# Products with V in a visit of their own, and the first block's loads and ScalarE order

## The chip, the cores and the metric

The kernel runs on one core of a Trainium2 chip. TensorE (PE) multiplies matrices into PSUM, VectorE (DVE) and ScalarE (ACT) do the elementwise work, GpSimd (POOL) and SyncE (SP) here only issue DMAs, which move data between HBM and SBUF or within SBUF. Each engine works through its own instructions in order and waits on semaphores for the others. The metric is device time in microseconds (us), the median of three runs: lower is better.

## The reference

Attention with a relative-position bias, then two gated feed-forward layers, all in float32, with 4 batches, 8 heads, 576 positions, head size 64, so 2304 tokens of 512:

```python
scores = scale * np.matmul(q, k.transpose(0, 1, 3, 2))
x = (psi_rel / psi_i)[..., None]          # logs of |i-j| and of i
bias = np.maximum(x @ w1 + b1, 0.0) @ w2  # hidden 32, then 8 heads
scores = scores + bias.transpose(2, 0, 1)[None, :, :, :]
scores = scores - np.max(scores, axis=-1, keepdims=True)
attn = np.exp(scores)
attn = attn / (np.sum(attn, axis=-1, keepdims=True) + 1e-09)
x = np.matmul(attn, v)                    # to 2304 x 512
x = (1 / (1 + np.exp(-(x @ w_gate))) * (x @ w_val)) @ w_out   # d_ff 1536
h = x @ w_in                              # d_ff 2048
out = (h * np.clip(h + 3.0, 0.0, 6.0) / 6.0) @ w_out2
```

## The kernel before

**Tiling.** The 576 query positions are cut into five chunks (`QC`): four of 128 and one of 64 positions, each with all four batches, so 512 tokens (256 in the last). For each chunk there is attention, done unit by unit (`units`), and a block of 68 weight steps (`STEPS`: G and V are the two halves of the first layer, Y its output, H and O the second layer). Attention of chunk c + 1 runs beside the weight steps of chunk c. A lead computes chunk 0's attention alone. A unit is one pair of heads and one batch (two batches in the last chunk).

**A weight step** (`moe_step`, `product`, L496) is 12 matmuls of 128x512: every operand is split into a high and a low float32r part, and three of the four cross products are summed. ScalarE and VectorE then make the gate and split the result again (L505, L507, L523, L527, L532, L533). Weights come from HBM, 512 KB a step (`w_load`, L422 in the first block, L426 later). In the first block they are also converted from packed float64 and split (`w_split`, L466 to L477) and stored for the later blocks (`w_store`, L482).

**Attention of chunks 2 to 4** goes by pairs of units. `pair_qk` computes the scores of both (L368, L374 in the last chunk). `pair_soft` adds the bias and finds the minimum of the negated scores (L390), exponentiates (L256), normalises (L269) and transposes 32x32 blocks into `t` (L295). `pair_turn` copies `t` into `pT` by sixteen DMAs (L305), from GpSimd, or in chunk 2 half of them from SP. `pair_av` multiplies with V (L326, 40 matmul records a pair), and `att_x` splits the sum (L346, L347). Attention of chunks 0 and 1 (`att_qk` to `att_av`, L231 to L326) transposes on TensorE instead (L282) and copies with ScalarE (L285).

**What sets the order.** `block` walks through the weight steps and calls the events of `block_events` that are due at or before a step. The events of chunk 1 come from `chunk_att`, those of chunks 2 to 4 from `chunk_pairs`, and the bias of the next chunks from `chunk_bias` (L124, L126 on ScalarE and VectorE, L135 on TensorE). TensorE takes its instructions in the order written, and in the lead and the first block SP does too. ScalarE and VectorE after the lead, and SP after the first block, are ordered by the framework's scheduler. `issue_after` (L624, L625) holds everything written after the lead behind one instruction on the named engine: `gate` is a V load on SP, `gate_act` an instruction on ScalarE.

**Buffers.** PSUM: two double banks for scores (`ps_s`), four banks for everything else (`ps_m`). In SBUF, after the first block: `k` 4, `v` 4, `s` 2, `t` 1, `pT` 1, weights `wp` 6, so a weight load can be at most six steps ahead.

Of the kernel before, what the change touches and what calls it, by code (L numbers as in the profile page):

```python
# [56 lines left out]
def fused_kernel(ctx: ExitStack, tc: tile.TileContext, qd, kd, vd, tz, rd, zc, w2b, iden, wpack, out):  # L57
# [215 lines left out]
    def att_tr(u, part, mm_ps):  # L273

        d = st[u]
        if part == 0:
            d["pt"] = A["pt"].tile([128, 9, NQ], F32, name="pT")
        p = d["s"].rearrange("p h j -> p (h j)")
        ps = mm_ps()
        for t in range(3):  # L280
            k = 3 * part + t
            nc.tensor.transpose(  # L282
                out=ps[:, t * NQ:t * NQ + NQ], in_=p[:, 128 * k:128 * k + 128], identity=id_t
            )
        issued[1] = nc.scalar.activation(  # L285
            out=d["pt"][:, 3 * part:3 * part + 3],
            in_=ps[:, 0:3 * NQ].rearrange("p (t n) -> p t n", t=3), func=AF.Copy,
        )
# [43 lines left out]
    def att_x(u, po=None):  # L332
# [10 lines left out]
                xy_p.tile([128, NTOK], F32R, name="xyl"),  # L343
            )
        xh, xl = (x[:, b * n:b * n + w] for x in xs[c, hp])
        nc.scalar.activation(out=xh, in_=po[:, 0:w], func=AF.Copy)  # L346
        nc.vector.tensor_tensor(out=xl, in0=po[:, 0:w], in1=xh.bitcast(F32), op=ALU.subtract)  # L347


# [215 lines left out]
    with ExitStack() as lead:  # L565
# [23 lines left out]
        for n in range(NL + 2):  # L589
# [19 lines left out]
                w_part((n - 4) // 6, (n - 4) % 6)  # L609
            if n == NL - 4:  # L610
                gate = issued[0]
            if n == NL - 1:
                gate_act = issued[1]

    def late(name, bufs):
# [29 lines left out]
    def chunk_att(c, t0, t1, lag):  # L645

        us = units[c]
        d = (t1 - t0) / (len(us) - 1 + lag)
        ev = [(t0 - 2 * d, lambda: att_load(us[0], False)), (t0 - d, lambda: bias_read(us[0]))]
        for i, u in enumerate(us):  # L650
            a = t0 + d * i

            def first(u=u, nxt=us[i + 1] if i + 1 < len(us) else None):
                if nxt:
                    load_rows(nxt)
                    load_k(nxt)
                att_qk(u)
                att_min(u)
                att_exp(u)
                att_norm(u)  # L660
# [5 lines left out]
            ev.append((a, first))  # L666
        return ev

    def chunk_pairs(c, t0, t1):

        us, fast = units[c], c in (2, 3)
        ps = [tuple(us[i:i + 2]) for i in range(0, len(us), 2)]
        d = (t1 - t0) / len(ps)
        ev = [(t0 - min(d, 8), lambda: [att_load(u) for u in ps[0]])]
        for i, p in enumerate(ps):
            a = t0 + d * i

            def first(p=p, prev=ps[i - 1] if i else None, nxt=ps[i + 1] if i + 1 < len(ps) else ()):
                if prev:
                    pair_av(prev)  # L680
                pair_qk(p)
                pair_soft(p, 0)
                for u in nxt:
                    att_load(u)

            ev.append((a, first))
            ev.append((a + 1.5, lambda p=p: pair_soft(p, 1)))
            if fast:
                ev.append((a - min(d / 2, 3), lambda p=p: [att_split(u) for u in p]))
        ev.append((t1, lambda: pair_av(ps[-1])))  # L690
        return ev

    def block_events(k):
        ev = []
        last = NSTEP - 1
        if k == 0:
            ev += chunk_bias(1, 2.0, 1.5, NG1)
            ev += chunk_att(1, 15.5, last, 2)
        elif k == 1:
            ev += chunk_bias(2, 2.0, 1.5)  # L700
            d = (last - 21.0) / 8
            ev += chunk_pairs(2, 21.0, last)
            ev += chunk_bias(3, 24.5 - d / 2 - 1 + d, d / 2)
        elif k + 1 < NC:
            ev += chunk_pairs(k + 1, 0.5, last)
            if k == 2:
                d = (last - 0.5) / 8
                ev += chunk_bias(4, 4.5 - d - 1 + d, d)
        return [e[::2] for e in sorted((e[0], n, e[1]) for n, e in enumerate(ev))]

    def block(k):
# [87 lines left out]
```

## Time and profile before

| what | value |
|---|---|
| median of 3 runs | 1185.09 us (1185.08 to 1187.76) |
| profiled execution | 1188.6 us, its span 1186.8 us |
| TensorE matmul busy | 1121.2 us (94% of the span) |
| VectorE busy | 681.4 us (57%) |
| ScalarE busy | 528.4 us (45%) |
| mean granted TensorE clock | 0.977 |
| mean rate of the DMA engines | 271 GB/s |

A share of busy time is a mean over stages. The stages here are the lead (0 to 92.1 us from the span's start) and the five blocks of weight steps, which start at 92.1, 354.4, 616.1, 874.7 and 1084.2 us. The profile names a wait after the instruction or DMA that ended it. A granted clock of 1.0 is 2.4 GHz, one of 0.5 is 1.2 GHz.

### The profile page before, as it was taken

Reading aid. Unit: us, or ns where it says so; the run is one execution under the profiler, and the core shown is the slowest. Engines: PE = TensorE matmul, PEld = TensorE weight load, DVE = VectorE, ACT = ScalarE, POOL = GpSimd, SP = SyncE. Lnnn points to the kernel's source line nnn. Section 1 sums busy time; section 2 is a strip of 40 time slices with the busy share of each in tenths; the row PEclk is TensorE's granted clock in tenths of the full one; section 3 lists DMA queues with packets and bytes.
Section 4 is the critical chain, followed back from the end, with each engine's and each line's share of the span. In section 5 each row is a group of like instructions: output and inputs, shape, how many; then the busy total and the mean of one; then the engine's idle time right before and its main releaser. Section 6 shows DMA issues by size and latency. Waiting matters only on the chain.

```text
span 1186.8 us, 20167 instructions
## 1 busy us (share of the span) xinstructions
PE 1121.2 (94%) x7316; PEld 907.0 (76%) x7316; DVE 681.4 (57%) x1536; ACT 528.4 (45%) x1042; POOL 127.7 (11%) x260
## 2 busy tenths in 40 slices
PE   7989989999999999989988988998899999999998
PEld 3767667777777777767767876877677887889998
DVE  7897898899844456875644644654442515341232
ACT  7786777788843334543412422433211303231231
POOL 0000000000000011122112222222212112020000
PEclk9899999999999999999999999998899999999999
DMA  6946999999877778878787878786679889687997
GB/s 207 343 168 246 341 389 396 348 337 378 306 260 249 250 238 265 280 220 280 254 261 224 269 220 262 215 247 187 186 233 281 263 241 284 205 235 258 360 369 273
DMA packets 126610, 321.25 MB, mean 271 GB/s; under 512 B 25520, under 2 KB 40240, under 8 KB 126512
## 3 DMA queue, kind: packets, MB, share of 16 engines
q1 hardware_dynamic: 117888, 300.99, 75.0%
q0 software_dynamic: 8192, 18.89, 6.1%
q8 instruction: 58, 0.95, 0.3%
q14 instruction: 40, 0.33, 0.1%
q10 hardware_dynamic: 432, 0.09, 0.0%
HBM read 244.73 MB, written 50.99 MB: 249 GB/s over the span
## 4 chain that ended last, share of the span: by engine, by line
PE 64%; DVE 12%; DMA 12%; issue 3%; SPq 2%; POOL 2%; ACT 2%; DVEq 0%; ACTq 0%; POOLq 0%
PE ps L496 45%; PE ps L326 9%; DMA pT<-t 8%; PE ps L231 3%; PE ps L282 3%; DVE t L295 3%; DVE s L390 3%; PE ps L135 3%; POOL pT L305 2%; SPq L305 2%; DMA wp<-wsp 2%; DVE s L269 2%; PE ps L368 2%; DMA wd<-wpack 2%; DVE kl L212 1%
## 5 line engine op out<-in xcount | busy, mean ns | idle before, releaser
L496 PE MATMUL ps<-xyh,wp 128*128 128x512 f32 (+1 forms) x1600 | 469.7, 373 | 6.3 <-DVE tmp L527 2.9
L496 PEld LDWEIGHTS ps<-xyh,wp 128*128 128x128 f32 x1600 | 292.0, 190 | 66.2 <-issue 6.7
L496 PE MATMUL ps<-gh,wp 128*128 128x512 f32 (+1 forms) x1120 | 330.1, 372 | 0.0
L496 PE MATMUL ps<-xyl,wp 128*128 128x512 f32 (+1 forms) x800 | 296.5, 371 | 0.7 <-DVE xyl L509 0.7
L496 PEld LDWEIGHTS ps<-gh,wp 128*128 128x128 f32 x1120 | 203.4, 189 | 38.6 <-issue 3.7
L305 POOL DMA_DIRECT2D pT<-t x256 | 127.5, 505 | 925.7 <-DVE tmp L527 458.8
L496 PE MATMUL ps<-gl,wp 128*128 128x512 f32 (+1 forms) x560 | 206.6, 369 | 0.2 <-DVE gl L507 0.2
L496 PEld LDWEIGHTS ps<-xyl,wp 128*128 128x128 f32 x800 | 151.9, 190 | 25.1 <-DVE xyl L509 1.4
L505 ACT ACTIVATE gh<-tmp 128x512 fp32r<-128x512 f32 (+1 forms) x140 | 82.4, 589 | 169.3 <-DVE tmp L527 118.8
L326 PE MATMUL ps<-pT,vt 128*64 128x128 f32 (+1 forms) x1600 | 105.9, 291 | 44.6 <-DMA pT<-t 33.3
L326 PEld LDWEIGHTS ps<-pT,vt 128*64 128x64 f32 x1600 | 93.0, 152 | 61.5 <-issue 51.2
L507 DVE TENSOR_TENSOR gl<-tmp,gh 128x512 fp32r<-128x512 f32 (+1 forms) x140 | 89.1, 636 | 61.5 <-ACT gh L505 61.4
L256 ACT ACTIVATE s<-s,m 128x576 f32<-128x576 f32 x144 | 110.4, 769 | 28.8 <-DVE m L390 20.0
L496 PEld LDWEIGHTS ps<-gl,wp 128*128 128x128 f32 x560 | 105.7, 189 | 17.1 <-DVE gl L507 0.9
L527 DVE SCALAR_TENSOR_TENSOR tmp<-tmp,ps 128x512 f32<-128x512 f32 (+1 forms) x60 | 37.8, 630 | 98.6 <-PE ps L496 97.3
L347 DVE TENSOR_TENSOR xyl<-ps,xyh 128x128 fp32r<-128x128 f32 (+1 forms) x52 | 17.7, 341 | 131.4 <-ACT xyh L346 131.3
L346 ACT ACTIVATE xyh<-ps 128x128 fp32r<-128x128 f32 (+1 forms) x52 | 16.5, 317 | 162.5 <-PE ps L326 162.3
L533 DVE SCALAR_TENSOR_TENSOR tmp<-tmp,ps 128x512 f32<-128x512 f32 (+1 forms) x80 | 50.4, 630 | 45.9 <-ACT tmp L532 44.3
L532 ACT ACTIVATE tmp<-ps 128x512 f32<-128x512 f32 (+1 forms) x80 | 44.1, 552 | 42.2 <-PE ps L496 41.3
L124 ACT ACTIVATE z<-tz_t,zc_t,sc_t 128x576 f32<-128x576 f32 x72 | 57.1, 859 | 8.1 <-PE ps L135 5.5
L523 ACT ACTIVATE tmp<-ps 128x512 f32<-128x512 f32 (+1 forms) x60 | 33.1, 552 | 57.7 <-PE ps L496 57.5
L295 DVE STREAM_TRANSPOSE t<-s 128x1152 f32<-128x1152 f32 x40 | 55.0, 1376 | 2.1 <-DVE r L263 1.5
(60 smaller groups left out, 1055.8 us busy)
## 6 DMA issues: line engine op xcount, KB each, us to landing
wp<-wsp SPq DMA_DIRECT2D x272, 512.0 KB, 5.4
wd<-wpack SPq DMA_DIRECT2D x68, 512.0 KB, 6.5
wsp<-wp SPq DMA_DIRECT2D x68, 512.0 KB, 5.6
vt<-vd SPq DMA_DIRECT2D x80, 320.0 KB, 5.1
kt<-kd SPq DMA_DIRECT2D x80, 288.0 KB, 4.8
pT<-t POOLq DMA_DIRECT2D x256, 72.0 KB, 5.3
biasD<-bo SPq DMA_DIRECT2D x18, 576.0 KB, 3.6
bm<-biasD SPq DMA_DIRECT2D x15, 576.0 KB, 4.7
```

Of the source, the lines that this page charges most:

```text
L124: nc.scalar.activation(out=z, in_=x, func=AF.Relu, scale=sc_t[:, t:t + 1], bias=b1c)
L135: nc.tensor.matmul(out=ps[32 * g:32 * g + 32, j, 0:NI], lhsT=w2b_t, rhs=z[:, g, NI * j:NI * j + NI], start=True, stop=True, tile_position= ...
L256: nc.scalar.activation(out=s[:, h], in_=s[:, h], func=AF.Exp, scale=-1.0, bias=d["m"][:, h:h + 1], accum_out=r[:, h:h + 1],)
L295: nc.vector.transpose(out=tn_q[0][:, :, x], in_=st[u]["s"].rearrange("p h j -> p (h j)").rearrange("p (t q j) -> p q t j", q=4, j=32),)
L305: (nc.sync if p[0][0] == 2 and i > 1 else nc.gpsimd).dma_start(out=pt[32 * q:32 * q + 32, i].rearrange("j u t i -> j (u t i)"), in_=t[32 * ...
L326: nc.tensor.matmul(out=po[64 * h:64 * h + 64, n * a:n * a + n], lhsT=vt[:, v], rhs=pt[:, m * a:m * a + m, k, :], start=(t == 0), stop=(t = ...
L496: nc.tensor.matmul(out=ps[:, 0:nt], lhsT=w[:, c, :], rhs=x[:, 0:nt], start=(first and c == 0 and i == 0), stop=(last and c == 3 and i == 2),)
L505: nc.scalar.activation(out=hi[:, 0:nt], in_=src, func=AF.Copy, scale=scale)
L507: nc.vector.tensor_tensor(out=lo[:, 0:nt], in0=src, in1=hi[:, 0:nt].bitcast(F32), op=ALU.subtract)
L527: nc.vector.scalar_tensor_tensor(out=th, in0=th, scalar=1.0, in1=ps, op0=ALU.add, op1=ALU.mult)
L532: nc.scalar.activation(out=t, in_=ps, func=AF.Relu, bias=3.0)
L533: nc.vector.scalar_tensor_tensor(out=t, in0=t, scalar=6.0, in1=ps, op0=ALU.min, op1=ALU.mult)
```

## The change

In `chunk_pairs` (chunks 2 to 4) the products with V are an event of their own, `lag` = 10 weight steps after the pair's scores. Before, `first` issued the previous pair's products, then its own scores. The spacing `d` of the pairs is now (`t1` - `lag` - `t0`) / 7 for eight pairs, / 3 for four; before, it was (`t1` - `t0`) / 8 or / 4. Loads are parted: the rows of Q and the bias and K of the next pair after the scores (`heads`), V after the products (`values`), in chunks 2 and 3 for the pair after next. `block_events` passes the lag and moves the bias of chunks 3 and 4 with it. In `chunk_att` (chunk 1, beside the first block) K and the rows are loaded two units ahead, not one. `gate_act` is now the ScalarE copy in `att_x` at lead iteration 16; before, it was the last copy in `att_tr` at iteration 15.

```diff
@@ -282,7 +282,7 @@
             nc.tensor.transpose(
                 out=ps[:, t * NQ:t * NQ + NQ], in_=p[:, 128 * k:128 * k + 128], identity=id_t
             )
-        issued[1] = nc.scalar.activation(
+        nc.scalar.activation(
             out=d["pt"][:, 3 * part:3 * part + 3],
             in_=ps[:, 0:3 * NQ].rearrange("p (t n) -> p t n", t=3), func=AF.Copy,
         )
@@ -343,7 +343,7 @@
                 xy_p.tile([128, NTOK], F32R, name="xyl"),
             )
         xh, xl = (x[:, b * n:b * n + w] for x in xs[c, hp])
-        nc.scalar.activation(out=xh, in_=po[:, 0:w], func=AF.Copy)
+        issued[1] = nc.scalar.activation(out=xh, in_=po[:, 0:w], func=AF.Copy)
         nc.vector.tensor_tensor(out=xl, in0=po[:, 0:w], in1=xh.bitcast(F32), op=ALU.subtract)


@@ -609,7 +609,7 @@
                 w_part((n - 4) // 6, (n - 4) % 6)
             if n == NL - 4:
                 gate = issued[0]
-            if n == NL - 1:
+            if n == NL:
                 gate_act = issued[1]

     def late(name, bufs):
@@ -646,11 +646,14 @@

         us = units[c]
         d = (t1 - t0) / (len(us) - 1 + lag)
-        ev = [(t0 - 2 * d, lambda: att_load(us[0], False)), (t0 - d, lambda: bias_read(us[0]))]
+        ev = [
+            (t0 - 2 * d, lambda: att_load(us[0], False)),
+            (t0 - d, lambda: (bias_read(us[0]), load_rows(us[1]), load_k(us[1]))),
+        ]
         for i, u in enumerate(us):
             a = t0 + d * i

-            def first(u=u, nxt=us[i + 1] if i + 1 < len(us) else None):
+            def first(u=u, nxt=us[i + 2] if i + 2 < len(us) else None):
                 if nxt:
                     load_rows(nxt)
                     load_k(nxt)
@@ -666,28 +669,40 @@
             ev.append((a, first))
         return ev

-    def chunk_pairs(c, t0, t1):
+    def chunk_pairs(c, t0, t1, lag):

         us, fast = units[c], c in (2, 3)
         ps = [tuple(us[i:i + 2]) for i in range(0, len(us), 2)]
-        d = (t1 - t0) / len(ps)
-        ev = [(t0 - min(d, 8), lambda: [att_load(u) for u in ps[0]])]
+        np_, ahead = len(ps), 2 if fast else 1
+        d = (t1 - lag - t0) / (np_ - 1)
+
+        def heads(i):
+            if i < np_:
+                for u in ps[i]:
+                    load_rows(u)
+                    load_k(u)
+
+        def values(i):
+            if i < np_:
+                for u in ps[i]:
+                    load_v(u)
+
+        ev = [(t0 - min(d, 8), lambda: heads(0)), (t0 - min(d, 8) + 0.1, lambda: values(0))]
         for i, p in enumerate(ps):
             a = t0 + d * i

-            def first(p=p, prev=ps[i - 1] if i else None, nxt=ps[i + 1] if i + 1 < len(ps) else ()):
-                if prev:
-                    pair_av(prev)
+            def first(i=i, p=p):
                 pair_qk(p)
                 pair_soft(p, 0)
-                for u in nxt:
-                    att_load(u)
+                heads(i + 1)
+                if i == 0 and ahead == 2:
+                    values(1)

             ev.append((a, first))
             ev.append((a + 1.5, lambda p=p: pair_soft(p, 1)))
+            ev.append((a + lag, lambda i=i, p=p: (pair_av(p), values(i + ahead))))
             if fast:
                 ev.append((a - min(d / 2, 3), lambda p=p: [att_split(u) for u in p]))
-        ev.append((t1, lambda: pair_av(ps[-1])))
         return ev

     def block_events(k):
@@ -697,15 +712,17 @@
             ev += chunk_bias(1, 2.0, 1.5, NG1)
             ev += chunk_att(1, 15.5, last, 2)
         elif k == 1:
+            lag = 10.0
+            d = (last - lag - 21.0) / 7
             ev += chunk_bias(2, 2.0, 1.5)
-            d = (last - 21.0) / 8
-            ev += chunk_pairs(2, 21.0, last)
-            ev += chunk_bias(3, 24.5 - d / 2 - 1 + d, d / 2)
+            ev += chunk_pairs(2, 21.0, last, lag)
+            ev += chunk_bias(3, 20.0 + lag - d / 2, d / 2)
         elif k + 1 < NC:
-            ev += chunk_pairs(k + 1, 0.5, last)
+            lag = 10.0
+            d = (last - lag - 0.5) / 7
+            ev += chunk_pairs(k + 1, 0.5, last, lag)
             if k == 2:
-                d = (last - 0.5) / 8
-                ev += chunk_bias(4, 4.5 - d - 1 + d, d)
+                ev += chunk_bias(4, lag - 0.5 - d, d)
         return [e[::2] for e in sorted((e[0], n, e[1]) for n, e in enumerate(ev))]

     def block(k):
```

Three places of the new order follow. The first is TensorE around scores and products of the third block: before, in its tenth weight step, where the products (L326, pT, vt) of the block's first pair stand right ahead of the scores (L368, kh, qh) of its second.

```order
L496 MATMUL ps_6690<-xyl_6219,wp_6581 128x512
L496 MATMUL ps_6690<-xyh_6218,wp_6581 128x512
L326 MATMUL ps_6705<-pT_6547,vt_6427 64x128 x10
L326 MATMUL ps_6705<-pT_6547,vt_6431 64x128 x10
L368 MATMUL ps_6730<-kh_6643,qh_6433 128x256
L368 MATMUL ps_6731<-kh_6643,qh_6433 128x256
```

After the change the same scores follow the weight matmuls directly.

```order
L496 MATMUL ps_6690<-xyh_6292,wp_6586 128x512
L496 MATMUL ps_6690<-xyl_6293,wp_6586 128x512
L496 MATMUL ps_6690<-xyh_6292,wp_6586 128x512
L368 MATMUL ps_6705<-kh_6643,qh_6433 128x256
L368 MATMUL ps_6706<-kh_6643,qh_6433 128x256
L368 MATMUL ps_6705<-kh_6643,ql_6434 128x256
```

And two weight steps later the products come by themselves, with the bias product (L135) of a later chunk behind them.

```order
L496 MATMUL ps_6788<-xyl_6293,wp_6623 128x512
L496 MATMUL ps_6788<-xyh_6292,wp_6623 128x512
L326 MATMUL ps_6829<-pT_6552,vt_6429 64x128 x10
L326 MATMUL ps_6829<-pT_6552,vt_6431 64x128 x10
L135 MATMUL ps_6858<-z_6538,w2b_t_95 32x288 x8
L135 MATMUL ps_6867<-z_6781,w2b_t_95 32x288 x8
```

The products moved behind two more weight steps and behind the next pair's scores.

The second place is SP in the second block, around the copies (L305) of the second pair; wp is a weight load, vt a V load, kt a K load, biasD a store of the bias. Before:

```order
L193 DMA kt<-kd 128x576
L185 DMA qt<-qd 128x4x128
L426 DMA wp<-wsp 128x1024 x2
L305 DMA pT<-t 32x576 x8
L426 DMA wp<-wsp 128x1024
L161 DMA biasD_87<-bo 128x2x576
L426 DMA wp<-wsp 128x1024 x2
L201 DMA vt<-vd 128x640 x2
L193 DMA kt<-kd 128x576
```

After:

```order
L426 DMA wp<-wsp 128x1024 x3
L201 DMA vt<-vd 128x640
L305 DMA pT<-t 32x576 x8
L201 DMA vt<-vd 128x640
L161 DMA biasD_87<-bo 128x2x576
L426 DMA wp<-wsp 128x1024
L193 DMA kt<-kd 128x576
L426 DMA wp<-wsp 128x1024
L193 DMA kt<-kd 128x576
L426 DMA wp<-wsp 128x1024 x4
```

The eight copies stand between the two V loads of a pair now, which wait for products with V; before, they stood between weight loads, ahead of the V loads.

The third place is ScalarE at the end of the lead: pT is the copy of transposed scores (L285), xyh the copy of a unit's sum (L346), cm and wp belong to the conversion of weights (L466, L476), z to the hidden layer of the bias (L124). Before:

```order
L285 ACTIVATE pT<-ps 128x384 x3
L466 ACTIVATE cm<-wd 128x512 x2
L124 ACTIVATE z<-tz_t,zc_t,sc_t 128x576 x4
L346 ACTIVATE xyh<-ps 128x128
L285 ACTIVATE pT<-ps 128x384 x3
L476 ACTIVATE wp<-cm 128x512 x2
L466 ACTIVATE cm<-wd 128x512
```

After:

```order
L285 ACTIVATE pT<-ps 128x384 x3
L346 ACTIVATE xyh<-ps 128x128
L285 ACTIVATE pT<-ps 128x384 x3
L346 ACTIVATE xyh<-ps 128x128
L466 ACTIVATE cm<-wd 128x512 x2
L124 ACTIVATE z<-tz_t,zc_t,sc_t 128x576 x4
L346 ACTIVATE xyh<-ps 128x128
L476 ACTIVATE wp<-cm 128x512 x2
L523 ACTIVATE tmp<-ps 128x512
```

Two copies of sums and one group of transposed copies moved ahead of the first conversion and the hidden layer; the last unit's sum is behind them.

## Rows read from the trace of the kernel before

**Rows 1.** Blocks one to four: us, busy PE, PEld, DVE, ACT, POOL, clock, DMA share, GB/s.
```profile
92.10:354.40 262.30, 256.36 (x1516) 198.19 (x1516) 219.46 (x447) 193.41 (x373) 0.00 (x0) 0.99 0.90 334
354.40:616.10 261.70, 243.71 (x1585) 193.88 (x1584) 152.13 (x348) 103.80 (x188) 32.54 (x64) 0.98 0.79 257
616.10:874.70 258.60, 235.33 (x1394) 193.59 (x1393) 127.02 (x304) 79.88 (x156) 63.48 (x128) 0.95 0.77 227
874.70:1084.20 209.50, 206.62 (x1265) 167.94 (x1264) 79.25 (x172) 53.06 (x100) 31.52 (x64) 0.99 0.80 247
```
**Rows 2.** Groups by line: L326, blocks two and three; busy, mean ns | idle, releasers.
```profile
L326 PE MATMUL ps<-pT,vt 128*64 128x128 f32 x320 | 23.6, 312 | 17.8 <-DMA pT<-t 10.0 <-DMA outT<-acc 5.2 <-DMA wp<-wsp 1.6
L326 PE MATMUL ps<-pT,vt 128*64 128x128 f32 x320 | 27.8, 348 | 23.3 <-DMA pT<-t 23.3
```
**Rows 3.** Timeline of TensorE, second to fourth block: start us, us, instruction [idle before].
```profile
490.73 0.38 PE L368 MATMUL ps<-kh,qh 64*128 64x256 f32 x2
492.52 0.51 PE L496 MATMUL ps<-xyh,wp 128*128 128x512 f32 x1
...
514.18 3.75 PE L326 MATMUL ps<-pT,vt 128*64 128x128 f32 x40 [5.48 <-DMA pT<-t]
...
809.30 0.58 PE L368 MATMUL ps<-kh,qh 64*128 64x256 f32 x2
...
839.10 4.54 PE L326 MATMUL ps<-pT,vt 128*64 128x128 f32 x40 [5.42 <-DMA pT<-t]
...
869.50 2.40 PE L326 MATMUL ps<-pT,vt 128*64 128x128 f32 x40 [1.35 <-DMA pT<-t]
...
877.50 2.17 PE L374 MATMUL ps<-kt,qt 64*64 64x256 f32 x32
```
**Rows 4.** Stretches at half clock, columns as in 1; the sum: eight, blocks two and three.
```profile
86.90:93.70 6.80, 5.22 (x35) 4.14 (x35) 5.51 (x12) 5.06 (x12) 0.00 (x0) 0.50 0.77 254
...
sum 34.10, PE 30.27 PEld 28.77 DVE 1.03 ACT 1.41 POOL 0.00; mean PE 3.78 PEld 3.60 DVE 0.13 ACT 0.18 POOL 0.00
```
**Rows 5.** Chain of waits, fourth block: start us, us, what.
```profile
1035.21 43.75 PE ps L496 x192
```
**Rows 6.** Line L305 on SP, second block: duration ns min/median/max, then landing.
```profile
L305 SPq DMA_DIRECT2D pT<-t x64: 507/588/1384, 432.5 to 604.8; - x64
...
DMA to landing us min/median/max: 1.9/3.4/6.9
```
**Rows 7.** Timeline of VectorE, second block.
```profile
498.89 1.37 DVE L295 STREAM_TRANSPOSE t<-s 128x1152 f32<-128x1152 f32 x1
...
504.69 1.37 DVE L295 STREAM_TRANSPOSE t<-s 128x1152 f32<-128x1152 f32 x1
```
**Rows 8.** Timeline of GpSimd, 885 to 910 us; landings there and at 693 to 712.
```profile
889.21 3.92 POOL L305 DMA_DIRECT2D pT<-t  x8 [25.41 <-DVE t L295]
...
901.24 0.99 POOL L305 DMA_DIRECT2D pT<-t  x2 [0.16 <-issue]
DMA to landing us min/median/max: 5.8/7.1/8.8
DMA to landing us min/median/max: 3.8/5.3/6.4
```
**Rows 9.** DMA issues on the page: KB each, median us to landing.
```profile
wp<-wsp SPq DMA_DIRECT2D x272, 512.0 KB, 5.4
```
**Rows 10.** Timeline of ScalarE at the end of the lead.
```profile
83.65 1.28 ACT L466 ACTIVATE cm<-wd 128x512 f32<-128x512 f32 x2
84.82 3.13 ACT L124 ACTIVATE z<-tz_t,zc_t,sc_t 128x576 f32<-128x576 f32 x4
```
**Rows 11.** Waits of TensorE, 84 to 180 us: in total, times, longest.
```profile
PE ps L326 <- DVE xyl L347: 3.6, 1, 3.6
PE ps L496 <- DVE tmp L527: 2.9, 1, 2.9
PE ps L231 <- DMA kt<-kd: 1.8, 1, 1.8
```

## The prediction

> **What bounds the kernel now.** I read the busy times by stage first. Four of the five blocks of weight steps stand in [rows 1]. TensorE is the engine that is nearly always at work: 256.4 of 262.3 us in the first block, 206.6 of 209.5 in the fourth. In the second and third it falls to 243.7 of 261.7 and 235.3 of 258.6, and there the granted clock is lowest too (0.98, 0.95). VectorE, ScalarE and the DMA engines are further from full in these two than in the first block (DMA share 0.79 and 0.77 against 0.90).
>
> Next, who ends TensorE's idle time there. In both blocks it is one line, L326, the products with V: 17.8 us of idle before it in the second block and 23.3 in the third [rows 2], 41.1 us together, all but 0.2 us of the idle time in them. The releaser is a landing DMA, by name pT<-t in most cases; where another DMA is named, it landed at the same moment as the pair's last copy.
>
> Then TensorE in order of time [rows 3]. A pair's scores (L368) start at 809.30, its products with V at 839.10 after 5.42 us of idle. TensorE arrives early and waits, so the 29.8 us between are the length of the chain from scores to products (minima, exponentials, normalising, two transposes, sixteen copies, landing). This is the longest of the eight pairs in the third block. In the second block, where half of the copies go through SP, the longest is 23.5 (490.73 to 514.18).
>
> Last, what a wait costs behind it. After some of them the granted clock falls to half, 0.50. There are eight such stretches in the two blocks, each beside a wait before products, and TensorE was busy 30.3 us in them (their sum in [rows 4]). At the other level that work takes half as long: 15.1 us are lost.
>
> **The change part by part.** *Products moved.* Before, the products of a pair stand right ahead of the next pair's scores; now they stand ten weight steps behind their own scores. A step is 12 matmuls; 192 take 43.75 us [rows 5], so 2.73 us a step and 27.3 for ten.
>
> In the third block the way from the start of the scores to the products is then the scores (1.8, from 490.73 to the next weight matmul at 492.52), ten steps, and the next pair's scores in between: 30.9 us, against chains of at most 29.8. All eight waits go, the worst with 1.1 us in hand.
>
> In the second block ten steps, two sets of scores and one of products (2.4, the row at 869.50) make 33 us against 23.5. But pT and t exist once. The copies now wait until the products of the pair before have read pT; those end five or six steps before the pair's own are due, 13.7 us at least. Eight copies on SP are issued in 8 x 0.59 us and land in a median 3.4 [rows 6], 8.1 us. The next transposes must wait for t as long, 8.1 us after a set of scores starts at the earliest; before, the first came at 498.89, 8.2 after its scores [rows 7]. So VectorE waits nothing there. Gains: 17.8 + 23.3, and with the waits the 15.1 us of half clock.
>
> In the fourth block nothing waits today, because a pair has 16 to 17 steps. Ten steps cut that to 2.2 + 27.3 = 29.5 us. The first pair's scores start at 877.50 [rows 3], its last copies are issued after 901.24 and land in a median 7.1 [rows 8]: 31 us, the longest of the four. Cost between 0 and 4 x 3.2 (1.5 and a clock dip of 1.7 for each); I take +1, since only the first comes so late.
>
> *V loaded later, K at the scores.* The loads are as many as before. In the second block SP now has a V load, eight copies, a V load and a bias store in a row, waiting for one pair's products, and a weight load behind them: eleven issues at 0.59 and 5.4 of landing [rows 9], 11.9 us. The step that needs it is six steps and a set of scores away, 18.2 us. Hidden with 6 us to spare; without that cover each us over it is one of TensorE per pair.
>
> *ScalarE held longer in the lead.* The last units' copies now come before the conversion of weights and the hidden layer of the bias. Before, L466 and L124 (1.28 + 3.13 us) came first [rows 10], and TensorE waited 3.6 us for the split behind them [rows 11], with half clock around it (5.2 busy in 86.9 to 93.7 [rows 4], 2.6 lost). What is late next: the copy of the very last unit stands behind those 4.4 us now, and the last quarter of the first product needs it. I put that wait at 2.5. Net -3.7.
>
> *K two units ahead.* One wait of 1.8 us for kt goes [rows 11]. But the conversion starts some 3 us later while TensorE arrives earlier, VectorE is 84% busy in this block [rows 1], and the wait of 2.9 for L527 may grow. Bounds for the first block: -8.0 (3.6 + 2.6 + 1.8, nothing late) and +6 (3 us of late weights, twice). I take -3.
>
> *Sum.* -17.8 - 23.3 - 15.1 + 1 - 3, and +4 for what fuller queues give back in the two blocks (between 0 and the 15 of the first rival; nearer to 0, the waits having a reserve): -54.2. The profiled execution took 1188.6 us (span 1186.8, 1.8 around it), so 1134.4. The median of the runs shown, 1185.09, is 3.5 us below that execution, so I forecast 1131 us.
>
> **Rivals.** *Late copies.* GpSimd waits for landings between its sixteen issues: the first eight went out from 889.21, the last two at 901.24, each landing after 5.8 to 8.8 us, against a median of 5.3 at 693 to 712 [rows 8]. If each of the two rounds took 1.8 us more, as there, the longest chain is 33.4 against 30.9, a wait of 2.5; with about half of that as the mean of eight pairs 8 us, 2 more in the fourth block and three dips of 1.7: 15 us, 1146. For it: the third block would do its DMA work, 0.77 of 258.6 us, in 225, a share of 0.89. Against: the first block runs at 0.90 and TensorE hardly waits.
> The Trainium skill ("DMA: Bandwidth & Descriptors", section "Issuing engines are not separate DMA queues") says that transfers of all issuing engines run on the same 16 DMA engines and interleave. By that rule a TensorE that takes its weights sooner lengthens the very copies that it waits for, and this rival's 1146 would come rather than 1131. The two landing medians agree with it in direction; this trace has no stretch at 0.89 with pair copies in the third block's manner.
>
> *Late weights.* SP's row of eleven DMAs holds the weight load back. One issue of a copy has taken up to 1.38 us [rows 6]; eight at that rate, three others at 0.59 and a landing of 8 make 20.8, 2.6 over those 18.2. Seven pairs at 2.6 and a dip of 1.7: 30 us, 1161. Against it: the median issue is 0.59.
>
> *The single buffers set the pace* (the side where it gets slower). The loop in the second block is: products of a pair end, copies of the next, t free, transposes of the one after (5.8 us from the first to the second [rows 7]), copies again: copies + 6 us, against a period of 18.3 us of TensorE's own work (5.14 steps, scores, products). With copies of 8.1 it is hidden. From 12.3 on it decides, because VectorE takes its instructions in order and behind transposes that wait for t stand the elementwise parts of the weight steps. Copies of 21 us, about what sixteen on GpSimd took at 889 to 908, would cost 7 x (21 + 6 - 18.3) + 7 x 1.7 = 73 us and give 1204. Against it: only eight copies stand on each queue in this block.
>
> *Nothing gained.* Each wait might only move with its visit. That needs 54 us of new waits; no row points to a place for them.
>
> **How the numbers follow.** Forecast 0.62, its own range 1122 to 1141 (first block -8 to +6, the rest a few us); late copies 0.18, late weights 0.09, single buffers 0.07, nothing gained 0.04. The first three are faster by over 0.3% (3.6 us, about what a measurement of this kernel can tell from no change); a point goes to slower for conversions late beyond the bound: 0.88. Within 0.3%: 0.04. Slower: 0.08. The range takes in the forecast's own, late copies and late weights at that price: 1119 to 1161, the lower end with no give-back and -8 in the first block.
>
> **What would show it.** Idle time before L326 in the second and third block falls from 41.1 to under 6 us; the clock there rises to 0.99 or more; the blocks take about 239 and 225 to 229 us, the first 255 to 262, the fourth 209 to 212. In the lead no wait of 3.6 us at L326. The prediction is wrong if L326 still waits for pT in most pairs of the third block (late copies), if L496 waits for wp in the second (late weights), or if VectorE idles before L295 until pT lands (single buffers); in the first block, if the idle time exceeds today's 5.9 us.

## The result and the profile after

The changed kernel takes 1122.72 us (median of 4 runs, 1118.98 to 1124.52); the kernel before takes 1185.09 on the same occasion. The ratio is 0.9466, 95% interval 0.9434 to 0.9499. The profiled execution took 1124.49 us, its span 1122.7. The forecast was 1131 us, its range 1119 to 1161.

The four blocks with attention beside the weight steps, columns as in [rows 1]:

```profile
85.23:341.87 256.64, 254.59 (x1515) 196.88 (x1515) 223.89 (x457) 199.37 (x383) 0.00 (x0) 1.00 0.92 343
341.87:582.08 240.21, 238.99 (x1585) 189.60 (x1584) 151.79 (x348) 103.13 (x188) 32.00 (x64) 1.00 0.85 281
582.08:807.98 225.90, 225.90 (x1394) 183.93 (x1392) 125.38 (x304) 80.23 (x156) 63.10 (x128) 1.00 0.88 260
807.98:1020.10 212.12, 207.81 (x1266) 168.47 (x1264) 77.57 (x172) 52.46 (x100) 31.43 (x64) 0.98 0.79 244
```

Against [rows 1] the lead is 6.9 us shorter, the first block 5.7, the second 21.5, the third 32.7; the fourth is 2.6 longer. In the third block TensorE is now busy for all of 225.90 us. The products with V in the second and third block, as in [rows 2]:

```profile
L326 PE MATMUL ps<-pT,vt 128*64 128x128 f32 x320 | 19.2, 275 | 0.1
L326 PE MATMUL ps<-pT,vt 128*64 128x128 f32 x320 | 19.2, 275 | 0.0
```

Of 41.1 us of idle time 0.1 is left, and the mean matmul record falls from 312 and 348 ns to 275, since no products run at half clock any more. One pair of the third block on TensorE, in the manner of [rows 3]:

```profile
744.58 0.39 PE L368 MATMUL ps<-kh,qh 64*128 64x256 f32 x2
...
752.01 2.40 PE L326 MATMUL ps<-pT,vt 128*64 128x128 f32 x40
770.93 0.39 PE L368 MATMUL ps<-kh,qh 64*128 64x256 f32 x2
...
778.39 2.40 PE L326 MATMUL ps<-pT,vt 128*64 128x128 f32 x40
```

The sixteen copies of this pair, first and last row of six:

```profile
755.96 0.50 POOL L305 DMA_DIRECT2D pT<-t  x1 [12.44 <-DVE xyl L347]
...
766.42 0.50 POOL L305 DMA_DIRECT2D pT<-t  x1 [0.23 <-issue]
```

The scores start at 744.58, their own products at 778.39. In these 33.8 us stand not only ten steps and the next pair's scores (770.93), but also the products of the pair before (752.01, 2.40 us). The last copies go out at 766.42 and landed at 772.6: a chain of 28.1 us with 5.8 in hand.

What TensorE still waits for in these four blocks, by line and releaser (total, times, longest); the first three rows are of the first block, then the second, then the fourth:

```profile
PE ps L496 <- DVE wp L477: 1.1, 1, 1.1
PE ps L496 <- ACT xyh L346: 0.8, 1, 0.8
PE ps L496 <- ACT pT L285: 0.2, 1, 0.2
PE ps L368 <- DVE bo L153: 1.1, 3, 0.4
PE ps L496 <- DMA wp<-wsp: 4.3, 1, 4.3
```

The waits of [rows 11] are gone. The largest of what is left is a weight load in the fourth block. Here is SP's queue ahead of it:

```profile
817.14 0.38 SPq L426 DMA_DIRECT2D wp<-wsp  x1
817.62 1.80 SPq L193 DMA_DIRECT2D kt<-kd  x4
819.47 0.59 SPq L185 DMA_DIRECT2D qt<-qd  x1
820.15 1.22 SPq L175 DMA_DIRECT2D bm<-biasD  x2
821.47 8.43 SPq L426 DMA_DIRECT2D wp<-wsp  x6
```

The stretch at half clock around the wait, columns as in [rows 1]:

```profile
832.15:838.98 6.83, 5.13 (x12) 4.10 (x13) 0.00 (x0) 0.00 (x0) 2.94 (x6) 0.50 1.04 315
```

K, queries and bias of the next pair, some 3.8 us of issues, go out ahead of the weights whose step waits until 833.85; these, issued at 821.47, landed at 833.7, 12.3 us later.

### The profile page after: what moved, and what is told of

It reads as the page before. It is cut to its first block, busy times and chain, and to the rows that moved or that the text cites. A ratio compares the mean times of both kernels' runs of the same rounds, so it can differ in the third digit from the quotient of the medians.

```text
span 1122.7 us, 20155 instructions
## 1 busy us (share of the span) xinstructions
PE 1101.5 (98%) x7316; PEld 888.2 (79%) x7316; DVE 676.6 (60%) x1536; ACT 527.3 (47%) x1042; POOL 126.7 (11%) x260
## 4 chain that ended last, share of the span: by engine, by line
PE 84%; DVE 5%; ACT 5%; DMA 3%; issue 2%; SPq 0%; ACTq 0%; DVEq 0%
PE ps L496 67%; PE ps L326 7%; PE ps L135 3%; PE ps L282 2%; PE ps L368 2%; PE ps L231 2%; DMA wp<-wsp 1%; ACT z L124 1%; ACT cm L466 1%; DVE wp L477 1%; ACT s L256 1%; DMA kt<-kd 1%; PE ps L374 1%; DMA bm<-biasD 1%; DVE cm L468 1%
## 5 line engine op out<-in xcount | busy, mean ns | idle before, releaser
L305 POOL DMA_DIRECT2D pT<-t x256 | 126.5, 501 | 881.2 <-DVE tmp L527 449.8
L256 ACT ACTIVATE s<-s,m 128x576 f32<-128x576 f32 x144 | 110.5, 769 | 28.2 <-DVE m L390 18.2
L527 DVE SCALAR_TENSOR_TENSOR tmp<-tmp,ps 128x512 f32<-128x512 f32 (+1 forms) x60 | 37.8, 631 | 100.9 <-PE ps L496 100.3
L326 PEld LDWEIGHTS ps<-pT,vt 128*64 128x64 f32 x1600 | 79.1, 137 | 16.4 <-issue 12.7
L326 PE MATMUL ps<-pT,vt 128*64 128x128 f32 (+1 forms) x1600 | 91.7, 266 | 0.1
L346 ACT ACTIVATE xyh<-ps 128x128 fp32r<-128x128 f32 (+1 forms) x52 | 16.4, 315 | 108.5 <-PE ps L326 108.5
L523 ACT ACTIVATE tmp<-ps 128x512 f32<-128x512 f32 (+1 forms) x60 | 33.1, 552 | 58.6 <-PE ps L496 58.5
L124 ACT ACTIVATE z<-tz_t,zc_t,sc_t 128x576 f32<-128x576 f32 x72 | 57.1, 858 | 7.1 <-PE ps L135 4.9
L509 DVE SCALAR_TENSOR_TENSOR xyl<-ps,xyh 128x512 fp32r<-128x512 f32 (+1 forms) x20 | 12.7, 634 | 72.2 <-ACT xyh L505 72.2
```

The source lines that it names most:

```text
L124: nc.scalar.activation(out=z, in_=x, func=AF.Relu, scale=sc_t[:, t:t + 1], bias=b1c)
L256: nc.scalar.activation(out=s[:, h], in_=s[:, h], func=AF.Exp, scale=-1.0, bias=d["m"][:, h:h + 1], accum_out=r[:, h:h + 1],)
L305: (nc.sync if p[0][0] == 2 and i > 1 else nc.gpsimd).dma_start(out=pt[32 * q:32 * q + 32, i].rearrange("j u t i -> j (u t i)"), in_=t[32 * ...
L326: nc.tensor.matmul(out=po[64 * h:64 * h + 64, n * a:n * a + n], lhsT=vt[:, v], rhs=pt[:, m * a:m * a + m, k, :], start=(t == 0), stop=(t = ...
L527: nc.vector.scalar_tensor_tensor(out=th, in0=th, scalar=1.0, in1=ps, op0=ALU.add, op1=ALU.mult)
```

## The experiments

Theory: the gain is the waits for the copies with the half clock behind them, and it comes from the distance between scores and products; the two edits of the first block add their own part. Rivals: the parts work only together; the moved loads or the separate visit are the gain; the single buffers `t` and `pT`, or weights queued on SP, set a new pace.

**The pair part alone.** The new `chunk_pairs` and `block_events`; `chunk_att` and the gate on ScalarE as before.

> Only the part of the change that concerns pairs (products in a visit of their own ten steps behind, V loaded at the products, K at the scores); the first block and the lead are as in the kernel before. Theory (the waits before the products and the half clock behind them are what was gained in the second and third block, and the first-block edits are worth their own 12.6 us beside it): lead and first block as before (first block starts at about 92 us and takes 262), second and third 240 and 226, together about 1122.7 + 12.6 = 1135 us. Rival (the two parts of the change work together, for instance a first block that ends otherwise shifts the second block's start): below 1128 or above 1142 us.

Measured: 1131.07 us, ratio 0.9522 (0.9494 to 0.9551). The second, third and fourth block:

```profile
352.14:592.33 240.19, 239.03 (x1586) 189.52 (x1585) 151.64 (x348) 103.16 (x188) 32.92 (x64) 1.00 0.85 280
592.33:818.22 225.89, 225.89 (x1394) 183.84 (x1392) 125.36 (x304) 80.26 (x156) 63.23 (x128) 1.00 0.88 260
818.22:1027.86 209.64, 206.85 (x1266) 167.69 (x1264) 77.53 (x172) 52.50 (x100) 31.46 (x64) 0.99 0.80 247
```

The two blocks are the changed kernel's to 0.02 us, with a lead and first block as of old (start at 89.5, 262.7 us long). So the 54 us of these blocks belong to this part alone, and the rest of the change is worth about 8 us, less than the 12.6 that the expectation took from the two first traces.

**The later gate alone, K alone, and both**, each on the kernel before:

```diff
-            if n == NL - 1:
+            if n == NL:
                 gate_act = issued[1]
```

and

```diff
-            def first(u=u, nxt=us[i + 1] if i + 1 < len(us) else None):
+            def first(u=u, nxt=us[i + 2] if i + 2 < len(us) else None):
```

> Only the later gate on ScalarE in the lead; K one unit ahead and the pairs as before. Theory: the wait of 3.57 us before L326 at 88.48 shrinks to about 0.8 before L496, the half clock around it goes, and the wait for L527 in the first block, which follows from where the conversions stand, goes too: first block starts at about 88 to 89 us (the other 3 us of the lead's 6.9 are half clock at 30 to 36 us, ahead of anything the change moves, and so chance of one execution) and takes 258 to 260; about 1185 - 6 = 1179 us. Rival (the wait of the last unit's copy only moves, and the conversions come late): no gain, 1185, with a wait of 2.5 us before L496 and over 3 us for L527.

> Only K two units ahead in the first block; the gate and the pairs as before. Theory: one wait of 1.78 us for kt goes and with it some half clock; the lead is as before (wait of 3.6 us before L326, which stays) and the wait for L527 stays at 2.9: about 1185 - 2.5 = 1182.5 us, the first block 260. Rival (K's place in the SP queue is what freed the weights and their conversion): the wait for L527 goes here too and the first block takes 256 to 257, about 1179 us.

> Both edits of the first block (later gate, K two units ahead), the pairs as before. Theory: the two add up: first block starts at about 88 us and takes 256 to 257, second and third block as before (262, 259): 1185 - 9 = 1176 us. With the kernel that has only the pair part at about 1135, the two together should make the whole change: 1185 - 1122.7 = 62.4 = 50 + 12. Rival (the first-block edits gain only in connection with the pairs): over 1182 us.

Measured: gate 1174.39 us, ratio 0.988 (0.9844 to 0.9916); K 1184.57, 0.9972 (0.9941 to 1.0003); both 1182.71, 0.9947 (0.9918 to 0.9975). TensorE's longest waits from 60 to 350 us with the gate alone:

```profile
PE ps L496 <- DVE wp L477: 1.9, 1, 1.9
PE ps L496 <- ACT xyh L346: 0.8, 1, 0.8
```

With K alone:

```profile
PE ps L326 <- DVE xyl L347: 3.6, 1, 3.6
PE ps L496 <- DVE wp L477: 1.7, 3, 0.7
```

The gate takes the wait before L326 away and starts the first block at 84.9 us, where the two kernels with the old gate have 89.5 and 91.2. In its trace each edit by itself removes the waits for L527 and for `kt`; the first block takes 258.5, 257.1 and, with both, 257.1 us. There the edits don't add up: for K the rival held, which had the wait for L527 go as well. What kept L527 late before is not shown.

Both together time worse than the gate alone, and the intervals don't overlap. By its number (over 1182 us) that is the rival of this run. In the trace of both the first block ends at 343.7 us, as with the gate alone (343.4), so the difference would have to lie in later blocks; but this trace is of the fastest of twelve runs (1172.48 us) and doesn't show it. These kernels have the same order on TensorE in the second and third block; on VectorE, ScalarE and SP, which the scheduler orders there, the order differs at several places. So neither chance nor an effect of the edits on that order is ruled out. How far the two blocks differ, here with both edits:

```profile
343.69:605.66 261.97, 241.97 (x1585) 192.78 (x1584) 151.94 (x348) 103.77 (x188) 32.36 (x64) 0.99 0.79 258
605.66:859.46 253.80, 231.12 (x1393) 189.79 (x1392) 126.97 (x304) 79.78 (x156) 63.25 (x128) 0.97 0.79 231
```

And with K alone:

```profile
348.29:616.45 268.16, 248.22 (x1585) 198.86 (x1584) 151.96 (x348) 103.76 (x188) 32.39 (x64) 0.96 0.77 251
616.45:879.57 263.12, 235.63 (x1393) 194.01 (x1392) 127.11 (x304) 79.85 (x156) 62.88 (x128) 0.95 0.77 225
```

Idle time is 42.7 and 47.4 us, the clock 0.99 and 0.97 against 0.96 and 0.95, and the two blocks differ by 15.5 us between the traces. So the size of the first-block part is read better from kernels without those waits, whose VectorE and ScalarE have the same order in these blocks: 1131.07 against the changed kernel's 1122.72, and 1121.59 in its later runs, 8.4 to 9.5 us.

**The distance put back.** 5.74, 8.31 and 16.6 steps, so that the products again stand just ahead of the next pair's scores; V is loaded just behind these scores, apart from K.

```diff
-            ev.append((a + lag, lambda i=i, p=p: (pair_av(p), values(i + ahead))))
+            ev.append((a + lag, lambda p=p: pair_av(p)))
+            ev.append((a + d + 0.1, lambda i=i: values(i + ahead)))
```

> The changed kernel with the products put back to the distance they had before (5.7, 8.3 and 16.6 steps, just ahead of the next pair's scores), V still loaded apart from K, both first-block edits kept. Theory (the distance is the gain): L326 waits for pT again, about 18 us in the second and 23 in the third block, with half clock behind the waits; these blocks take about 262 and 254 to 263 us, the whole 1122.7 + 20 + 30 = about 1173 us. Rival (the loads at other places, or the products as an event of their own, are the gain): the two blocks stay within 5 us of 240 and 226, and the whole below 1140 us.

Measured: 1204.17 us, ratio 1.0187 (1.0139 to 1.0234). L326 in the second and third block:

```profile
L326 PE MATMUL ps<-pT,vt 128*64 128x128 f32 x320 | 28.0, 351 | 33.5 <-DMA pT<-t 20.6 <-DMA outT<-acc 7.1 <-DMA wp<-wsp 5.7
L326 PE MATMUL ps<-pT,vt 128*64 128x128 f32 x320 | 30.0, 368 | 28.8 <-DMA pT<-t 28.8
```

All the waits are back, with half clock (the blocks take 283.2 and 266.6 us). The rival that credits the moved loads falls. It came 31 us above the expectation, 21 of these in the second block, which lies in more than distance: V's loads and the bias of the next chunk stand at other places there than before. TensorE's order shows a good part of it:

```profile
481.90 2.40 PE L326 MATMUL ps<-pT,vt 128*64 128x128 f32 x40 [1.30 <-DMA pT<-t]
484.24 2.15 PE L135 MATMUL ps<-z,w2b_t 128*32 128x288 f32 x32
486.31 0.39 PE L368 MATMUL ps<-kh,qh 64*128 64x256 f32 x2
```

Four such bias products (L135) stand between a pair's products and the next scores here. In the kernel before they stand between scores and products (one at 477.93, scores at 467.77, products at 488.39). So four pairs have 2.15 us less work on the way to their products, 8.6 of the 15.7 us by which the idle time before L326 grew in this block (17.8 to 33.5). What V's loads cost was not tried.

**A quarter of a step more.** The changed kernel with 6 and 8.5 steps in the second and third block. The pairs stand 5.71 and 8.29 steps apart, so the products now come just behind the next pair's scores.

```diff
-            lag = 10.0
+            lag = 6.0          # third block: 8.5
```

> The changed kernel with 6 and 8.5 steps in the second and third block (pairs stand 5.71 and 8.29 steps apart there, so the products now fall just behind the next pair's scores); ten in the fourth. Theory (a visit in between counts, not the steps alone): against the kernel with 5.7 and 8.3 steps only a quarter of a step is added in name, but the next pair's scores and the products of the pair before, with a bias in the second block, now stand between: way in the third block 28 to 31 us against chains of 26 to 32, waits of 1 to 3 us in about three pairs; second block way 25 us against chains of 19 to 26, waits of 0 to 2 in three pairs; together 10 us with half clock behind: 1128 to 1140 us. Rival (the distance in steps is what counts): within 15 us of the 1204 of the kernel with 5.7 and 8.3 steps.

Measured: 1134.95 us, ratio 0.9566 (0.9531 to 0.9601), in the theory's range, with fewer pairs that wait than it said (two in the second block, one in the third), and with four waits before the bias product (L135), which it didn't name. The second and third block:

```profile
343.67:592.25 248.58, 241.76 (x1586) 191.18 (x1584) 150.11 (x348) 103.44 (x188) 31.95 (x64) 0.99 0.82 269
592.25:823.43 231.18, 226.71 (x1393) 185.72 (x1392) 126.06 (x304) 79.56 (x156) 63.13 (x128) 0.99 0.86 258
```

TensorE's longest waits in them:

```profile
PE ps L135 <- DVE m L390: 4.8, 4, 2.5
PE ps L326 <- DMA outT<-acc: 3.5, 1, 3.5
PE ps L326 <- DMA pT<-t: 2.2, 1, 2.2
```

69 us lie between this kernel and the one above, for a quarter of a step in name: the waits before L326 fall from 62.3 us to 6.2. V's loads stand with the products again, too, but the chain from scores to the last landing is no shorter for it in the third block (28.1 us in the mean of eight pairs, 28.2 above). What was gained there is that other visits lie in between. The 69 us are not all the worth of that place: the kernel above is itself about 20 us slower than the kernel before, which has the same distance. The two blocks take 549.7 us above and 479.8 here, 520.3 in the kernel before and 515.8 with both first-block edits, so the place behind the next visit is worth 36 to 70 us, by what it is compared with.

**8, 9 and 12 steps.** `lag` = 8, 9 and 12 in the second, third and fourth block.

> The changed kernel with 8, 9 and 12 steps in place of ten in the second, third and fourth block. Theory, corrected: what counts is that the products pass the next pair's scores (and the products of the pair before come between), which they do from 5.6 steps on in the second and from 8.2 on in the third block; the way there is then 28 to 31 us in the second and 31 in the third block against chains of 19 to 28 and 26 to 31: idle time before L326 under 5 us in both, blocks 240 and 226 to 229, the whole 1119 to 1128 us. Rival (the way as the prediction counted it, 30.9 us in the third block at ten steps with 1.1 us in hand): at nine 28.2, so the longer chains wait, 1.5 to 3 us in half of the pairs with half clock behind: third block 234 to 240, the whole 1132 to 1138 us.

Measured: 1122.5 us, ratio 0.9482 (0.945 to 0.9515), the same as with ten. The third block:

```profile
583.24:808.96 225.72, 225.72 (x1394) 183.87 (x1393) 125.07 (x304) 80.07 (x156) 62.75 (x128) 1.00 0.88 264
```

No wait at all, although the way is 28.5 to 33.1 us there and each pair's last copy lands 0.3 to 5.6 us ahead of its products. The prediction's count, by which a step less makes half of the pairs wait, was wrong.

**12, 12 and 14 steps.** `lag` = 12, 12 and 14.

> The changed kernel with 12, 12 and 14 steps. Theory of the single buffers: in the second block the products now fall behind the scores of the pair after the next; the copies of a pair start only when the products of the pair before have read pT, and t is free 8 us later, which is about 16 us after the scores of the pair whose transposes need it: L295 waits about 8 us a pair, VectorE holds the elementwise parts of the weight steps behind it, TensorE waits 1 to 4 us for them in six pairs, with half clock behind: the second block takes 250 to 270 us, the whole 1133 to 1150 us; third and fourth block as with ten steps. Rival (VectorE has enough in hand and TensorE runs on): 240 us in the second block, the whole 1119 to 1125 us.

Measured: 1122.88 us, ratio 0.9475 (0.9439 to 0.951). The scores of a pair of the second block on TensorE:

```profile
460.41 0.39 PE L368 MATMUL ps<-kh,qh 64*128 64x256 f32 x2
```

The transposes of the same pair on VectorE:

```profile
484.17 2.64 DVE L295 STREAM_TRANSPOSE t<-s 128x1152 f32<-128x1152 f32 x2
```

The transposes come 23.8 us after their scores, later than the 16 expected, and yet the block takes 241.9 us. VectorE's order is the scheduler's, which puts elementwise parts of the weight steps ahead of them. VectorE does idle before three of the transposes (4.8, 1.4 and 0.8 us), and once TensorE waits behind that. VectorE, then TensorE:

```profile
543.29 2.64 DVE L295 STREAM_TRANSPOSE t<-s 128x1152 f32<-128x1152 f32 x2 [1.36 <-DMA wp<-wsp]
546.56 0.50 PE L496 MATMUL ps<-xyh,wp 128*128 128x512 f32 x1 [1.87 <-DVE tmp L533]
```

So the theory's mechanism exists, with one wait of 1.9 us and not six of 1 to 4; the rival stated for this run held for the time.

**All copies on GpSimd** in the second block, with ten steps:

```diff
-                (nc.sync if p[0][0] == 2 and i > 1 else nc.gpsimd).dma_start(
+                nc.gpsimd.dma_start(
```

> The changed kernel with all sixteen copies of a pair on GpSimd in the second block too (none on SP), so that copies there last about 16 us from first issue to last landing, not 8. Prediction's loop of the single buffers (copies and then 6 us to the second transpose, against 18.3 us of TensorE's own work): 22 against 18.3, a wait of 3.7 us and a dip of 1.7 in seven pairs, 38 us more: about 1160 us. Theory corrected by the kernel with 12 steps (both units' exponentials are long done, so the two transposes need 2.7 us and no more behind the release of t; pairs come every 20.6 us at first and every 16 to 18 at the end): 18.7 us, waits of 1 to 2.5 us in the last three or four pairs only: 1125 to 1136 us.

Measured: 1130.3 us, ratio 0.9526 (0.9495 to 0.9558). The second block:

```profile
342.44:591.72 249.28, 240.60 (x1585) 191.15 (x1584) 151.95 (x349) 103.42 (x188) 64.81 (x128) 0.99 0.87 273
```

TensorE's waits in it:

```profile
PE ps L326 <- DMA pT<-t: 6.7, 3, 3.6
PE ps L368 <- DVE bo L153: 2.0, 4, 1.0
```

The last three pairs wait, 1.4 to 3.6 us each (1 to 2.5 expected), and their transposes come within 0.2 us of the landing of the copies before, as the corrected loop says. The block is 9.1 us longer. So the single buffers can set the pace, but at a fraction of the price that the prediction put on them.

**K later in the fourth block**, tied behind six more weight loads on SP:

```diff
+        def behind(i):
+            with tc.issue_after(issued[2].ins):   # the last w_load
+                heads(i)
-                heads(i + 1)
+                if fast:
+                    heads(i + 1)
+            if not fast:
+                ev.append((a + 6, lambda i=i: behind(i + 1)))
```

> The changed kernel, and in the fourth block K, queries and bias of the next pair loaded behind six more weight loads, not ahead of them. Theory (the wait of 4.3 us before L496 at 833.85 is a weight load queued behind K, queries and bias on SP, and the 6.8 us of half clock are its echo): the wait falls under 1 us, the half clock goes, the fourth block takes 204 to 206 us instead of 212, the whole 1115 to 1117 us. Rival (the wait comes from transfers of many kinds at once at the block's start, whatever the order on SP): the wait stays at 3 us or more and the block at 210 or more.

> The changed kernel once more, for comparison on one chip with the kernel that has the later loads: 1119 to 1125 us, with the wait of about 3 to 4 us before L496 in the fourth block, a block of 209 to 212 us.

Measured: 1118.11 us (1117.25 to 1120.18), ratio 0.9447 (0.9419 to 0.9475). The changed kernel once more, on a later occasion: 1121.59 us (1118.87 to 1124.5), 0.9448 (0.9422 to 0.9475). The fourth block with K later:

```profile
808.63:1014.16 205.53, 205.53 (x1265) 166.94 (x1264) 77.50 (x172) 52.49 (x100) 31.35 (x64) 1.00 0.81 256
```

The changed kernel's again:

```profile
808.31:1018.33 210.02, 206.88 (x1266) 167.69 (x1265) 77.50 (x172) 52.46 (x100) 31.39 (x64) 0.99 0.79 247
```

The wait and the half clock are gone, as the theory has it, but that the queue on SP alone made them is not shown. With SP's order of the changed kernel the wait varies: 4.3 and 3.1 us in its two traces, 0.7 with all copies on GpSimd, 0.8 with 6 and 8.5 steps. It goes with the time from issue to landing of the first weight load behind K, queries and bias (12.3, 10.5 and 9.2 us in the first three of these), and K later moves their transfers as well as their issues, so this run doesn't part the theory from its rival. The kernel before, which has this order too (landing after 9.6 us), has the wait as well:

```profile
PE ps L496 <- DMA wp<-wsp: 2.2, 1, 2.2
```

So the block that wins 6.6 us against the first trace of the changed kernel wins 4.5 against its second and 0.9 against the kernel with all copies on GpSimd, where it took 206.4 us.

**Both together**, K later and 8, 9 and 12 steps:

> The later loads in the fourth block (K, queries and bias behind six more weight loads) together with 8, 9 and 12 steps. Theory: the fourth block takes 204 to 206 us (its wait of 4.3 and the half clock gone), the second 239.6 (three waits of 0.4 for a bias gone), the others as in the changed kernel: 1115 to 1119 us, 4 to 7 below the changed kernel's own time on the same chip. Rival (the fourth block's wait is chance): no difference beyond 2 us.

Measured: 1120.96 us (1119.95 to 1125.27), ratio 0.9456 (0.9428 to 0.9483), beside the changed kernel's 1121.59 on the same chip. The forecast gain of 4 to 7 us did not come; the rival, no difference beyond 2 us, fits. The fourth block took 207.0 us, and at nine steps the third block's first pair waited 0.5 us here. The traces with K later are shorter (spans of 1117.1 and 1118.2 us against 1122.7 and 1121.0), but that either version beats the changed kernel is not shown in the times.

## Why the prediction was right

**Waits and half clock.** Held. In the second and third block the idle time fell by 40.0 us, from 41.2 to 1.2 (1.1 of it the waits for L153) and TensorE's busy time by 14.2 (243.71 to 238.99 and 235.33 to 225.90), together 54.2. The terms were 41.1 and 15.1, less 4 given back. One reading was off: where another DMA than a copy ended a wait in the second block, it landed 0.5 to 0.9 us after the pair's last copy, not with it. The 15.1 was one draw: the four traces with the old pairs, with 41 to 47 us of idle time, have 23.9 to 51.2 us of these blocks at half clock, of which half, 12 to 26, is lost.

**The reserve in the third block.** The count was too low, and it was luck that the error lay on the safe side. The prediction had 30.9 us between scores and products; there are 31.2 to 35.9, because for all pairs but the first the products of the pair before, and in places a bias, stand in between as well. The longest chain was 31.1 us (scores at 718.2, landing at 749.3) and would have waited 0.2 with 30.9; it has 2.7 in hand.

**Late copies.** Did not come. The chain's mean over the eight pairs was 28.0 us and is 28.2, its longest 29.8 and now 31.1; the rival wanted 33.4. The DMA share did rise to 0.88, near the 0.89 that it counted on, and yet the copies of the third block land as fast as before. Before, then after:

```profile
DMA to landing us min/median/max: 2.6/5.4/7.4
DMA to landing us min/median/max: 1.8/5.5/7.6
```

From a pair's first issue to its last landing it is 15.5 us in the mean before and 15.4 after. The Trainium skill's rule ("DMA: Bandwidth & Descriptors", section "Issuing engines are not separate DMA queues"), that all issuers share the same 16 engines, stood behind this rival. No lengthening by it shows here, and 4 for what fuller queues give back was too much. In the rival's sum half of 2.5 us for eight pairs is 10 us, where it put 8.

**The second block.** That nothing is late there held, but not for the reason given. The copies do wait for `pT`, and transposes come up to 11.9 us after the scores. So this step came out right by luck. The rival's mechanism, VectorE held in order behind them, cost TensorE one wait of 1.9 us in the kernel at 12 steps; what is left of it is the loop of copies and two transposes, priced at 9 us by the kernel with all copies on GpSimd, where the prediction's way of counting gives 38.

**Late weights.** None in the second block. There is one in the fourth, where K, queries and bias go out ahead of a weight load. The prediction took it that nothing waits there today, but the kernel before waits 2.2 us for `wp` at the same place. It put its +1 there on the copies; 2.6 was measured, and 0.5 in the second trace, both with a longer wait for `wp` (4.3 and 3.1) and none for `pT`.

**Lead and first block.** The mis-sized term: -3 forecast, -12.6 between the two traces, -8.4 to -9.5 between medians. Three things make up most of it. The wait for the last unit's copy was put at 2.5 and is 0.76. The late conversions (up to +6) did not come (waits for L477 are 1.1 us, 1.0 before); the wait of 2.9 for L527 went instead, with the 3.4 us at half clock behind it. And the trace of before had a stretch at half clock in the lead, ahead of all that the change moves, which the trace after lacks:

```profile
28.87:35.70 6.83, 6.83 (x25) 4.17 (x24) 4.27 (x14) 4.31 (x11) 0.00 (x0) 0.50 1.02 368
```

It stands in two of the later traces too, at 28.65 with both first-block edits and at 28.80 with 6 and 8.5 steps, so it is chance, and 3.4 us (half of 6.83) are no gain of the change. The forecast of 1131 us was right within 8.3 us because the terms of the two large blocks were.

## What to carry to other kernels

Count what stands between a producer and its consumer in the order of the engine that waits, visits of other work included: here the first place behind the next visit, a quarter of a step on, was worth 36 to 70 us. Beyond the longest chain more distance bought nothing here, and the single buffers cost 9 us only where their own loop was longer than the period (2.3 us of idle time at 12 steps). A small edit is measured in a kernel whose waits are gone, since the waits and the half clock behind them vary more from run to run than the edit gives.

## What was unexpected on the hardware

The half clock behind the waits varies from one execution to the next, and the times with it: the kernel before ran between 1176.89 and 1195.06 us over its runs here, the changed kernel between 1118.87 and 1124.52. And a short wait can be enough: with 6 and 8.5 steps one wait of 2.21 us, the only one before L326 in the third block, had this behind it:

```profile
622.71:626.13 3.42, 3.23 (x31) 3.26 (x33) 3.35 (x11) 2.34 (x6) 0.00 (x0) 0.50 0.61 156
```

Not each such wait has it: with both first-block edits a wait of 2.71 us at 883.74 in the fourth block left the granted clock at 1.00.
